# An attention and mixture kernel on one core: a new table of phase positions, and SyncE's queue for every transfer

## The chip, the core and the metric

The kernel runs on one core of one Trainium2 chip. The core has five engines with instruction streams of their own: TensorE (PE in the profile; its weight loads, PEld, overlap its products), VectorE (DVE), ScalarE (ACT), GpSimd (POOL) and SyncE (SP). Transfers are issued by an engine into a queue of its own and carried by 16 DMA engines. The metric is the device time of one execution in microseconds, as a median of several.

## The reference

A gated linear attention (4 batches, 8 heads, 768 positions, head size 48) feeds a two-matrix feed-forward with a gate:

```
scale = minimum(mag, 0.999) / (mag + 1e-6)          # mag = |a|, a = a_re + i a_im, per position and channel
for t in range(S):
    S_re, S_im = ar*S_re - ai*S_im + k[t] v[t]^T,  ar*S_im + ai*S_re
    y[t] = q[t] @ S_re
x = y, heads side by side                           # 4 x 768 x 384
xk, xr = mu * x + (1 - mu) * x_prev                 # one mu for each
v = relu(xk @ w_k)**2 @ w_v                         # 384 -> 1024 -> 384
out = sigmoid(xr @ w_r) * v                         # w_r 384 x 384
```

All is float32 at the interface; w_k, w_v and w_r arrive as eight bytes a number.

## The kernel before

The 4 x 768 positions are cut into eight units of 384, two to a batch. Each unit goes through three stages.

- `gate(u)`, on ScalarE and VectorE: it loads the unit's gates, keys and queries (g: three tiles, each of 128 channels by four rows of 384; six pieces of two rows for units 0 and 1) and its values (v, three tiles). From the gates it makes the running sum of log magnitude and of phase (`a0`, `a1`, `a2` for the magnitude: logarithms and exponentials on ScalarE, a scan, L736, on VectorE; `b0`, `b1` for the phase, with arctangent and sines). It multiplies keys and queries by both (L797). Unit 0 does that in two groups of tiles, the others in one. L719 (`a1`) is VectorE's step between two ScalarE steps on the magnitude.
- `attend(u)`, on TensorE: heads are stacked into kq by small transfers (`stack`, L834), scores (sc, L914) are masked on VectorE (pt, L923), keys transposed (tr, L865) and copied by ScalarE (kt, L871), and a state is updated (up, L885; added on VectorE, L890). The result y goes to SBUF by ScalarE (ys, L964) and by 48-row transfers to X (xt, L970, `move`).
- `mix(u)`, the feed-forward: VectorE makes the two mixtures x of neighbouring positions, TensorE the first products z (L455 for unit 0, which takes plain float32, L460 for the others, which take three products of split float32), ScalarE relu and square, its output split in hhi and hlo, and TensorE the second products o (L524, L527). The gate's z (`gate_r`) is copied by ScalarE (L478), goes through the sigmoid, is multiplied with o on VectorE (L542) and stored (L545).

The weights come in ten pieces, the first of one matrix block and the others of two (`fetch`, L380). Each is converted from its eight bytes by a step on ScalarE or VectorE (f0, L589 on ScalarE), a light pass on VectorE (L595) and a merge on VectorE (L599); `split` later divides them into the two parts that mix(1) and later units use.

The order of all this is set by a planner, class `Plan`. Each stage registers its operations with an engine, a cost in us and the buffers it uses. `due` goes over TensorE's operations sorted by a position, `at`, adds up their costs, and works back through the dependences to a due time for each operation of any engine. `run` then plays the program through: whenever an engine is free it takes, of the operations that can go, the one with the earliest due time. Instructions are emitted in that order, engine by engine, and at run time wait for one another by semaphores. When TensorE has nothing to do in the opening (from the first gate product that can't start to the first z), the planner puts fillers on it, `warm`, two matmuls each on the identity. Positions come from a table `AT` with a pair (start, end) for attend(u) and one for mix(u), in that order:

```
for u in range(NU):
    run(attend(u), *AT[2 * u])
    run(mix(u, (x0, x0_slot) if u == 0 else None), *AT[2 * u + 1])
```

so only the order of the positions over all steps matters, not their scale. Queues of transfers are engines to the planner: `SP`, SyncE's, and `GP`, GpSimd's, each with an issue cost (`QUEUE`) and, if not free at once, a time from which it is (`FREE`). `op_dma`, `op_move` and `op_dma_gp` register a transfer on SP, on whichever of both is free, or on GP.

Of the kernel before, what the change touches and what calls it, by code (L numbers as in the profile page):

```python
# [23 lines left out]
P = 128  # L24
U = 384
NC = U // P
NU = B * S // U
NT = C // P
# [13 lines left out]
CAP = 0.999  # L42


AT = ((0.42, 0.67), (2.23, 4.26), (0.93, 2.49), (2.73, 3.06), (2.24, 2.87), (3.78, 4.38), (2.83, 3.48), (4.03, 5.22),
      (3.96, 4.06), (5.16, 6.45), (5.4, 5.45), (9.16, 9.34), (6.35, 8.61), (9.06, 11.24), (9.26, 9.59), (9.6, 10.3))
PAIRS = 0, 3, 1, 2
PIECE = 2
GP = 2
# [22 lines left out]
class Plan:  # L72
# [8 lines left out]
    BEGIN = 0.8  # L81
    LATENCY = 0.16
    TABLE = 1.28
    QUEUE = dict(SP=0.63, GP=0.65)
    FREE = dict(GP=2.4, DVE=6.5)
    START, ARRIVE = 1.15, 1.3
    TURN = {("once", "half"): 0.09, ("full", "half"): 0.09,
            ("half", "once"): 0.24, ("half", "full"): 0.15}
# [189 lines left out]
def tile_kernel(ctx, tc, gat, vt, w_all, mu, slow_g, slow_v, out):  # L278
# [54 lines left out]

    def op_move(n, f, **kw):

        plan[0].op("SP", n / 220, lambda e: f(nc.sync if e == "SP" else nc.gpsimd), other={"GP": n / 220}, **kw)

    def op_dma_gp(n, f, **kw):

        plan[0].op("GP", n / 400, f, **kw)  # L340


    table(AF.Ln)
# [207 lines left out]
    with ExitStack() as fast:  # L551
# [14 lines left out]
        def fetch(i):  # L566
            s = pieces[i]
            n = s.stop - s.start

            def f():  # L570
                raws[i] = fetched(keep, s, nc.sync if i >= FETCHED else nc.gpsimd, tag=f"w{i}")[0]
            late = i >= FETCHED
            (op_dma if late else op_dma_gp)(393 * n, f, writes=[("raw", i)], reads=[("kqs", 0, ct) for ct in range(NT)] * late, bulk=late)

        def convert(i):

# [71 lines left out]
        def gate(u):  # L648
# [9 lines left out]
            def load(ct, part):  # L658
                def f():
                    if u not in G:  # L660
                        G[u] = gp.tile([P, NT, 4, U], F32, tag="g", name="g")
                    (nc.gpsimd if u == 1 else nc.sync).dma_start(out=G[u][:, ct, part], in_=gat[b, half, ct, :, part])
                key = ("in", u, ct, part.stop)
                (op_dma_gp if u == 1 else op_dma)(
                    196.6 * (part.stop - part.start), f, writes=[("g", u, ct, i) for i in range(part.start, part.stop)] + [key],
                    uses=[g_slot[u]], bulk=u >= FIRST_LOAD)

            def load_v(c):
                def f():
                    v = ap.tile([P, C + C // 2], F32, tag="v", name="v", bufs=VB)  # L670
                    (nc.sync if u else nc.gpsimd).dma_start(out=v, in_=vt[b, half, c])
                    V[u].append(v)
                (op_dma if u else op_dma_gp)(295, f, writes=[("v", u, c)], uses=[v_slot[u][c]])

            def each(c):
                return range(c.start, c.stop)
# [136 lines left out]
        def attend(u):  # L813
# [6 lines left out]
            def stack(h):  # L820
                extra = u == 0 and len(kq) - KQ
                if u == 0 and extra >= 0:

                    kq_slot[h], kq[h] = x0_slot, x0[:HR + D, NT - 2 + extra]
                else:
                    kq_slot[h] = slot("kq")
                    kq[h] = kqs[kq_slot[h][1] % KQ]
                r0, r1 = h * D, (h + 1) * D

                def move(r0, n, i):  # L830
                    def f():
                        ct, o = r0 // P, r0 - h * D
                        s = slice(r0 - ct * P, r0 - ct * P + n)
                        nc.sync.dma_start(  # L834
                            out=kq[h][i * HR + o:i * HR + o + n], in_=G[u][s, ct, 2 * i:2 * i + 2])
                    plan[0].op("SP", n * 3.07 / 220, f, reads=[("kqs" if i else "kqc", u, r0 // P)], writes=[("st", u, h, i, r0)],
                           uses=[kq_slot[h], g_slot[u]])
# [89 lines left out]
            def values(p):  # L927
# [38 lines left out]
                op_act(U + 60, out_, reads=[("y", u, p)], writes=[("ys", u, p)], uses=[sp, sy])  # L966

                def move(src, dst, i):
                    def f(queue):
                        queue.dma_start(out=X[u][dst, i, 1:U + 1], in_=t["ys", p][src])  # L970
                    k = (src.stop - src.start) * 1.54
                    (op_move if u == 0 else lambda k, f, **kw: plan[0].op("SP", k / 220, lambda: f(nc.sync), **kw))(k, f, reads=[("ys", u, p), ("X0", u)], writes=[("Xp", u, i, dst.start)],
                           uses=[sy, x_slot[u]])
# [196 lines left out]
```

## Time and profile before

| | |
|---|---|
| median of 3 runs | 432.51 us (432.43, 432.51, 433.48) |
| profiled execution, device time | 431.53 us |
| its span, first to last instruction | 429.8 us |
| mean granted TensorE clock | 0.996 |
| TensorE busy | 383.5 us (89%) |
| ScalarE, VectorE, GpSimd busy | 340.7, 332.1, 19.9 us |

The trace covers the span; the device time of the same execution is 1.7 us more. A row of time gives start, length, engine, line, operation, what is written and read, the count, and in square brackets the idle time ahead of it with what ended it. A row of a stretch gives its bounds and length, then busy time and count of PE, PEld, DVE, ACT and POOL, granted clock, the mean busy share of the DMA engines and GB/s. A row of waits gives the waiting engine, its tile and line, what it waited for, the sum in us, the count and the mean. A row of transfers has tiles, queue, count, KB each and the median us from issue to landing.

### The profile page before, as it was taken

To read this page: it belongs to the slowest core of one execution; us is meant where nothing else is said; L and a number is where in the kernel's file an instruction comes from. 1 tells how busy PE (TensorE), PEld (TensorE's weight loads), DVE (VectorE), ACT (ScalarE), POOL (GpSimd) and SP (SyncE) were. 2 spreads that over 40 slices of the span, in tenths; PEclk is the share of its full clock that TensorE was granted. 3 is DMA by queue.
4 is the path that set the end of the run, shared out by engine and by line. 5 is a ranking of instruction groups with operands and counts; after the bars stand their busy time and mean duration, and the time that the engine had idled before them with its cause. 6 is when DMAs were issued, how large, how long until landed. Compare 5 with 4: busy or idle time off the path is not lost.

```text
span 429.8 us, 9500 instructions
## 1 busy us (share of the span) xinstructions
PE 383.5 (89%) x3683; PEld 350.8 (82%) x3683; DVE 332.1 (77%) x528; ACT 340.7 (79%) x606; POOL 19.9 (5%) x59
## 2 busy tenths in 40 slices
PE   1006999999999999989999999999999999998993
PEld 1005996676679998989999999999999999998993
DVE  6699799978598989599979899696959993456322
ACT  5698769967799898899999899987998964574530
POOL 7200111000000000000000000000000200000000
PEclk9999999999999999999999999999999999999998
DMA  7946897645726737582846582388353474314001
GB/s 265 410 204 161 280 324 242 111 93 225 206 58 179 269 87 156 155 297 76 186 135 219 208 183 75 80 297 211 108 137 115 109 181 126 110 37 130 1 2 63
DMA packets 27909, 69.92 MB, mean 163 GB/s; under 512 B 5696, under 2 KB 11664, under 8 KB 27856
## 3 DMA queue, kind: packets, MB, share of 16 engines
q1 hardware_dynamic: 26320, 62.15, 49.6%
q0 software_dynamic: 1536, 7.08, 4.2%
q8 instruction: 31, 0.51, 0.5%
q14 instruction: 22, 0.18, 0.2%
HBM read 40.90 MB, written 4.72 MB: 106 GB/s over the span
## 4 chain that ended last, share of the span: by engine, by line
PE 60%; DVE 13%; issue 10%; ACT 7%; DMA 7%; POOL 2%; SPq 0%; DVEq 0%; ACTq 0%; POOLq 0%
PE z L460 23%; PE o L527 15%; PE sc L914 4%; PE y L949 4%; PE z L455 4%; PE o L524 3%; PE y L955 3%; DMA g<-in_gat 2%; PE up L885 2%; DMA kq<-g 2%; ACT sq L302 2%; DVE g L797 1%; DVE ph L764 1%; PE tr L865 1%; DMA xt<-ys 1%
## 5 line engine op out<-in xcount | busy, mean ns | idle before, releaser
L460 PE MATMUL z<-x,w 128*128 128x384 f32 x693 | 132.0, 340 | 1.2 <-ACT r L496 1.0
L460 PEld LDWEIGHTS z<-x,w 128*128 128x128 f32 x693 | 120.5, 188 | 3.3 <-issue 1.4
L527 PE MATMUL o<-hhi,w 128*128 128x384 f32 x336 | 87.5, 341 | 0.0
L527 PEld LDWEIGHTS o<-hhi,w 128*128 128x128 f32 x336 | 60.0, 188 | 1.1 <-issue 0.7
L527 PE MATMUL o<-hlo,w 128*128 128x384 f32 x168 | 56.7, 338 | 1.7 <-DVE hlo L508 1.7
L496 ACT ACTIVATE r<-z 128x384 f32<-128x384 f32 x64 | 30.8, 485 | 24.3 <-PE z L460 22.1
L865 PE MATMUL tr<-ident,g 128*128 128x128 f32 x120 | 19.2, 286 | 33.7 <-DVE g L797 33.7
L797 DVE TENSOR_TENSOR g<-g,r 128x768 f32<-128x768 f32 x48 | 43.5, 952 | 3.1 <-ACT r L302 3.0
L865 PEld LDWEIGHTS tr<-ident,g 128*128 128x128 f32 x120 | 14.2, 144 | 36.4 <-DVE g L797 34.7
L914 PEld LDWEIGHTS sc<-kq 112*64 112x64 f32 x744 | 33.5, 137 | 4.9 <-issue 2.5
L914 PE MATMUL sc<-kq 112*64 112x128 f32 (+1 forms) x744 | 36.6, 250 | 0.5 <-DMA kq<-g 0.4
L318 DVE CAST hhi<-h 128x384 fp32r<-128x384 f32 x34 | 12.2, 359 | 28.2 <-PE o L527 17.5
L500 ACT ACTIVATE h<-r 128x384 f32<-128x384 f32 x64 | 33.4, 525 | 0.7
L527 PEld LDWEIGHTS o<-hlo,w 128*128 128x128 f32 x168 | 31.5, 188 | 2.0 <-DVE hlo L508 2.0
L923 DVE TENSOR_TENSOR pt<-sc,masks 128x512 int32<-128x512 int32 x48 | 31.1, 681 | 1.6 <-PE sc L914 1.6
L302 ACT ACTIVATE sq<-m 128x1152 f32<-128x1152 f32 (+2 forms) x27 | 27.8, 1054 | 5.3 <-DVE m L745 2.8
L508 DVE TENSOR_TENSOR hlo<-h,hhi 128x384 fp32r<-128x384 f32 x56 | 30.6, 551 | 1.5 <-ACT hhi L318 0.2
L442 DVE TENSOR_TENSOR x<-xm,x 128x384 fp32r<-128x384 f32 x42 | 22.7, 552 | 10.7 <-ACT x L439 10.6
L296 ACT ACT_TABLE_LOAD x22 | 28.2, 1283 | 1.2 <-PEq L1159 0.8
L949 PE MATMUL y<-pt,v 128*48 128x128 f32 (+1 forms) x384 | 28.2, 277 | 0.2 <-DVE pt L923 0.2
L753 DVE TENSOR_TENSOR g<-g,sq 128x768 f32<-128x768 f32 x24 | 21.8, 952 | 5.4 <-ACT sq L302 5.2
L431 DVE SCALAR_TENSOR_TENSOR xm<-dx,mu_sb,xt 128x384 f32<-128x384 f32 x42 | 25.0, 614 | 0.8
(90 smaller groups left out, 657.7 us busy)
## 6 DMA issues: line engine op xcount, KB each, us to landing
g<-in_gat SPq DMA_DIRECT2D x18, 768.0 KB, 6.2
kq<-g SPq DMA_DIRECT2D x94, 144.0 KB, 3.5
again<-in_w_all SPq DMA_DIRECT2D x19, 384.0 KB, 3.3
v<-in_vt SPq DMA_DIRECT2D x21, 288.0 KB, 3.8
out_t<-zr SPq DMA_DIRECT2D x24, 192.0 KB, 2.0
raw<-in_w_all SPq DMA_DIRECT2D x5, 768.0 KB, 6.5
xt<-ys SPq DMA_DIRECT2D x45, 72.0 KB, 2.2
raw<-in_w_all POOLq DMA_DIRECT2D x4, 768.0 KB, 9.1
```

The costliest lines, as they stand in the source:

```text
L296: nc.scalar.add_instruction(mybir.InstLoadActFuncSet(name=nc.get_next_instruction_name(), act_func_set_id=loaded[0], engine=mybir.EngineTy ...
L302: nc.scalar.activation(out=out, in_=in_, func=func, **kw)
L460: nc.tensor.matmul(z, lhsT=wt[s[0]][:, part, s[1]], rhs=r[which][:, ct], start=n == 0, stop=n == 3 * NT - 1)
L496: nc.scalar.activation(out=t["r", j], in_=t["f", j], func=AF.Relu)
L500: nc.scalar.activation(out=t["h", j], in_=t["r", j], func=AF.Square)
L508: nc.vector.tensor_tensor(out=t["lo", j], in0=t["h", j], in1=t["hi", j].bitcast(F32), op=ALU.subtract)
L527: nc.tensor.matmul(tiles["o", mt], lhsT=wt[W_V + 2 * j][:, part, ts(mt, P)], rhs=r, start=j == 0 and n == 0, stop=j == NJ - 1 and n == 2)
L797: nc.vector.tensor_tensor(out=g[:, ct, 2 * i:2 * i + 2], in0=g[:, ct, 2:4], in1=t["r"][:, ct, 1 - i:2 - i].to_broadcast([P, 2, U]), op=ALU ...
L865: nc.tensor.transpose(out=t["tr", c, part][:, ct * P:(ct + 1) * P], in_=G[u][:, ct, 2 * part, c * P:(c + 1) * P], identity=ident)
L914: nc.tensor.matmul(sc[rows, i, cols], lhsT=kq[2 * p + j][:, 0, c * P + late * Q:][:, :Q], rhs=q if j else q[:, ::-1], start=True, stop=True)
L923: nc.vector.tensor_tensor(out=pts[k, c].bitcast(I32), in0=both, in1=masks.unsqueeze(1).to_broadcast([P, 2, 2, P]), op=ALU.bitwise_and)
L949: nc.tensor.matmul(t["y", p][rows, ts(c, P)], lhsT=V[u][c][:, cols], rhs=w, start=c == 0, stop=False)
```

## The change

Three things change. `AT` has other numbers, from a search over them. The queue `GP` is gone: `op_dma_gp` is removed, and its users (the g of unit 1, the v of unit 0, the first five pieces of weights) take `op_dma`, SP's. `op_move` has SP alone, so that the X transfers of unit 0, half of which GpSimd could issue, are all SyncE's. The computation is the same.

```
-AT = ((0.42, 0.67), (2.23, 4.26), (0.93, 2.49), (2.73, 3.06), (2.24, 2.87), (3.78, 4.38), ...
+AT = ((2.35, 6.85), (3.56, 5.8), (0.03, 4.77), (13.51, 15.8), (6.77, 9.94), (22.02, 23.4), ...
-    QUEUE = dict(SP=0.63, GP=0.65)
-    FREE = dict(GP=2.4, DVE=6.5)
+    QUEUE = dict(SP=0.63)
+    FREE = dict(DVE=6.5)
...
     def op_move(n, f, **kw):
-        plan[0].op("SP", n / 220, lambda e: f(nc.sync if e == "SP" else nc.gpsimd), other={"GP": n / 220}, **kw)
-
-    def op_dma_gp(n, f, **kw):
-        plan[0].op("GP", n / 400, f, **kw)
+        plan[0].op("SP", n / 220, f, **kw)
...
         def fetch(i):
...
-                raws[i] = fetched(keep, s, nc.sync if i >= FETCHED else nc.gpsimd, tag=f"w{i}")[0]
+                raws[i] = fetched(keep, s, nc.sync, tag=f"w{i}")[0]
             late = i >= FETCHED
-            (op_dma if late else op_dma_gp)(393 * n, f, writes=[("raw", i)], ...
+            op_dma(393 * n, f, writes=[("raw", i)], ...
...
             def load(ct, part):
...
-                    (nc.gpsimd if u == 1 else nc.sync).dma_start(out=G[u][:, ct, part], in_=gat[b, half, ct, :, part])
+                    nc.sync.dma_start(out=G[u][:, ct, part], in_=gat[b, half, ct, :, part])
...
             def load_v(c):
...
-                    (nc.sync if u else nc.gpsimd).dma_start(out=v, in_=vt[b, half, c])
+                    nc.sync.dma_start(out=v, in_=vt[b, half, c])
...
                 def move(src, dst, i):
-                    def f(queue):
-                        queue.dma_start(out=X[u][dst, i, 1:U + 1], in_=t["ys", p][src])
+                    def f():
+                        nc.sync.dma_start(out=X[u][dst, i, 1:U + 1], in_=t["ys", p][src])
```

After the change lines from 337 on stand four lower, those from 966 on five lower (L719 becomes L715, L1009 becomes L1004). What moves is shown at three places. In the rows, a name is the tile that is written, then `<-` and what is read.

First, the opening of the queues. Before, this is the head of SyncE's transfers (kq_97 and kq_98 are the first stacked heads):

```order
L370 DMA mu_sb<-in_mu 128x6
L662 DMA g<-in_gat 128x768 x6
L671 DMA v<-in_vt 128x576
L834 DMA kq_97<-g 48x768
L834 DMA kq_98<-g 48x768
```

and this all of GpSimd's transfers, ahead of its copies of the last position:

```order
L662 DMA g<-in_gat 128x768 x6
L671 DMA v<-in_vt 128x576 x3
L380 DMA raw<-in_w_all 128x6144 x2
L380 DMA raw<-in_w_all 128x3072
L380 DMA raw<-in_w_all 128x6144 x2
L970 DMA xt<-ys 48x384
L970 DMA xt<-ys 32x384
L970 DMA xt<-ys 16x384
L970 DMA xt<-ys 48x384 x2
L988 COPY last<-xt 128x3 x4
```

After, the head of SyncE's:

```order
L366 DMA mu_sb<-in_mu 128x6
L658 DMA g<-in_gat 128x768 x12
L376 DMA raw<-in_w_all 128x6144 x4
L376 DMA raw<-in_w_all 128x3072
L667 DMA v<-in_vt 128x576 x4
L830 DMA kq_97<-g 48x768
L830 DMA kq_98<-g 48x768
```

The twelve pieces of g stand behind each other on one queue, the five pieces of weights behind them, and the four of v, which stood ahead of the weights, behind those.

Second, ScalarE and VectorE ahead of the scans of unit 1, while TensorE works on the attention of unit 0. ScalarE before, from the first exponential of unit 1 to the step ahead of its scans:

```order
L302 ACTIVATE ph,stat<-m 128x1152
L871 COPY kt<-tr 128x8x48 x2
L715 ACTIVATE sq,stat<-ph 128x3x384
L871 COPY kt<-tr 128x8x48
L302 ACTIVATE sq<-sq 128x3x384
L871 COPY kt<-tr 128x8x48
L302 ACTIVATE sq<-m 128x3x384
L871 COPY kt<-tr 128x8x48
L302 ACTIVATE sq<-sq,consts 128x3x384
L726 ACTIVATE m<-m,consts 128x1152
```

and after:

```order
L302 ACTIVATE ph,stat<-m 128x1152
L867 COPY kt<-tr 128x8x48
L618 CAST w<-raw 128x2x384
L867 COPY kt<-tr 128x8x48
L711 ACTIVATE sq,stat<-ph 128x3x384
L302 ACTIVATE sq<-sq 128x3x384
L867 COPY kt<-tr 128x8x48 x2
L302 ACTIVATE sq<-m 128x3x384
L302 ACTIVATE sq<-sq,consts 128x3x384
L722 ACTIVATE m<-m,consts 128x1152
```

One copy of kt of five moved behind the scans' last input, none stands between the square and its logarithm any more, and a cast of a weight piece came in. VectorE before, over the same time:

```order
L703 SCALAR_TENSOR_TENSOR ph<-ph,g 128x1152
L599 SCALAR_TENSOR_TENSOR raw<-raw 128x768
L892 COPY state_95<-up 112x384
L599 SCALAR_TENSOR_TENSOR raw<-raw 128x768
L923 TENSOR_TENSOR pt<-sc,masks 128x512 x2
L719 SCALAR_TENSOR_TENSOR m<-sq,m 128x1152
L923 TENSOR_TENSOR pt<-sc,masks 128x512
L890 TENSOR_TENSOR state_96<-up,state_95 112x384
L736 SCALAR_TENSOR_TENSOR m<-m,stat,sq 128x384 x3
```

and after:

```order
L699 SCALAR_TENSOR_TENSOR ph<-ph,g 128x1152
L591 TENSOR_SCALAR raw<-raw 128x384
L621 TENSOR_TENSOR w<-raw,w 128x2x384
L595 SCALAR_TENSOR_TENSOR raw<-raw 128x384
L888 COPY state_95<-up 112x384
L715 SCALAR_TENSOR_TENSOR m<-sq,m 128x1152
L919 TENSOR_TENSOR pt<-sc,masks 128x512 x3
L886 TENSOR_TENSOR state_96<-up,state_95 112x384
L732 SCALAR_TENSOR_TENSOR m<-m,stat,sq 128x384 x3
```

Masks of scores (pt) that stood ahead of L719 stand behind it (L715 now), and two merges of weights gave way to smaller weight steps.

Third, TensorE's end, with the numbers of the tiles (o has three, one for each 128 columns; n is the one-column product of the flag that guards the slow path, and `good` comes from VectorE). Before:

```order
L527 MATMUL o_4615<-hhi_4767,w_1300 128x384 x2
L527 MATMUL o_4615<-hlo_4779,w_1300 128x384
L1041 MATMUL n_4877<-consts_82,good_4875 1x1
L527 MATMUL o_4607<-hhi_4793,w_1367 128x384 x2
L527 MATMUL o_4607<-hlo_4805,w_1367 128x384
L527 MATMUL o_4611<-hhi_4793,w_1367 128x384 x2
L527 MATMUL o_4611<-hlo_4805,w_1367 128x384
L527 MATMUL o_4615<-hhi_4793,w_1367 128x384 x2
L527 MATMUL o_4615<-hlo_4805,w_1367 128x384
```

with the last gate product z four rows ahead of the first of these. After:

```order
L523 MATMUL o_4619<-hhi_4774,w_1416 128x384 x2
L523 MATMUL o_4619<-hlo_4786,w_1416 128x384
L523 MATMUL o_4623<-hhi_4774,w_1416 128x384 x2
L523 MATMUL o_4623<-hlo_4786,w_1416 128x384
L456 MATMUL z_4822<-x_4474,w_1486 128x384 x3
L456 MATMUL z_4822<-x_4474,w_280 128x384 x6
L1036 MATMUL n_4871<-consts_82,good_4869 1x1
```

A gate product z is now the last large work of TensorE, behind the last o; the load of the flag on SyncE, `L1040 TENSOR_LOAD bad`, stands ahead of the last store, where it stood ahead of the last three.

More of the change, by code (lines that the diff above doesn't have):

```diff
@@ L42 @@
 CAP = 0.999
-AT = ((0.42, 0.67), (2.23, 4.26), (0.93, 2.49), (2.73, 3.06), (2.24, 2.87), (3.78, 4.38), (2.83, 3.48), (4.03, 5.22),
-      (3.96, 4.06), (5.16, 6.45), (5.4, 5.45), (9.16, 9.34), (6.35, 8.61), (9.06, 11.24), (9.26, 9.59), (9.6, 10.3))
+AT = ((2.35, 6.85), (3.56, 5.8), (0.03, 4.77), (13.51, 15.8), (6.77, 9.94), (22.02, 23.4), (14.62, 18.64), (22.27, 25.46),
+      (22.65, 22.92), (23.6, 25.31), (29.45, 44.63), (22.76, 34.84), (22.83, 25.16), (41.11, 56.64), (43.88, 61.13), (40.05, 48.46))
 PAIRS = 0, 3, 1, 2
@@ L570, in f @@
             def f():
-                raws[i] = fetched(keep, s, nc.sync if i >= FETCHED else nc.gpsimd, tag=f"w{i}")[0]
+                raws[i] = fetched(keep, s, nc.sync, tag=f"w{i}")[0]
             late = i >= FETCHED
-            (op_dma if late else op_dma_gp)(393 * n, f, writes=[("raw", i)], reads=[("kqs", 0, ct) for ct in range(NT)] * late, bulk=late)
+            op_dma(393 * n, f, writes=[("raw", i)], reads=[("kqs", 0, ct) for ct in range(NT)] * late, bulk=late)
         def convert(i):
@@ L661, in f @@
                         G[u] = gp.tile([P, NT, 4, U], F32, tag="g", name="g")
-                    (nc.gpsimd if u == 1 else nc.sync).dma_start(out=G[u][:, ct, part], in_=gat[b, half, ct, :, part])
+                    nc.sync.dma_start(out=G[u][:, ct, part], in_=gat[b, half, ct, :, part])
                 key = ("in", u, ct, part.stop)
-                (op_dma_gp if u == 1 else op_dma)(
+                op_dma(
                     196.6 * (part.stop - part.start), f, writes=[("g", u, ct, i) for i in range(part.start, part.stop)] + [key],
@@ L670, in f @@
                     v = ap.tile([P, C + C // 2], F32, tag="v", name="v", bufs=VB)
-                    (nc.sync if u else nc.gpsimd).dma_start(out=v, in_=vt[b, half, c])
+                    nc.sync.dma_start(out=v, in_=vt[b, half, c])
                     V[u].append(v)
-                (op_dma if u else op_dma_gp)(295, f, writes=[("v", u, c)], uses=[v_slot[u][c]])
+                op_dma(295, f, writes=[("v", u, c)], uses=[v_slot[u][c]])
             def each(c):
@@ L835, in f @@
                             out=kq[h][i * HR + o:i * HR + o + n], in_=G[u][s, ct, 2 * i:2 * i + 2])
-                    plan[0].op("SP", n * 3.07 / 220, f, reads=[("kqs" if i else "kqc", u, r0 // P)], writes=[("st", u, h, i, r0)],
+                    op_move(n * 3.07, f, reads=[("kqs" if i else "kqc", u, r0 // P)], writes=[("st", u, h, i, r0)],
                            uses=[kq_slot[h], g_slot[u]])
@@ L968, in move @@
                 def move(src, dst, i):
-                    def f(queue):
-                        queue.dma_start(out=X[u][dst, i, 1:U + 1], in_=t["ys", p][src])
-                    k = (src.stop - src.start) * 1.54
-                    (op_move if u == 0 else lambda k, f, **kw: plan[0].op("SP", k / 220, lambda: f(nc.sync), **kw))(k, f, reads=[("ys", u, p), ("X0", u)], writes=[("Xp", u, i, dst.start)],
-                           uses=[sy, x_slot[u]])
+                    def f():
+                        nc.sync.dma_start(out=X[u][dst, i, 1:U + 1], in_=t["ys", p][src])
+                    op_move((src.stop - src.start) * 1.54, f, reads=[("ys", u, p), ("X0", u)], writes=[("Xp", u, i, dst.start)],
+                            uses=[sy, x_slot[u]])
                     x_parts.setdefault(i, []).append(("Xp", u, i, dst.start))
```

## The prediction

> **What bounds the kernel now.** I read the page's busy shares first, then busy time by stretch, then what TensorE waited for once it had started, then the rows of time for the opening and the end.
>
> ```profile
> PE 383.5 (89%) x3683; PEld 350.8 (82%) x3683; DVE 332.1 (77%) x528; ACT 340.7 (79%) x606; POOL 19.9 (5%) x59
> ```
>
> ```profile
> 32.30:67.80 35.50, 31.94 (x422) 30.49 (x423) 30.69 (x42) 26.66 (x40) 4.97 (x6) 1.00 0.83 259
> ...
> 190.00:380.00 190.00, 189.62 (x1868) 181.59 (x1867) 154.38 (x257) 163.69 (x305) 3.60 (x14) 1.00 0.53 149
> 380.00:423.20 43.20, 41.55 (x237) 40.63 (x235) 19.27 (x41) 20.41 (x44) 0.00 (x0) 1.00 0.14 42
> 423.20:429.80 6.60, 0.01 (x1) 0.00 (x0) 0.67 (x2) 0.00 (x0) 0.00 (x0) 0.76 0.29 98
> ```
>
> Columns: stretch, length, busy PE, PEld, DVE, ACT, POOL, granted clock, DMA share, GB/s. TensorE has next to nothing to do before 32.3 (none of it from 4 to 20, in the stretches shown further down). From there to 67.8 it works on the attention of unit 0, and much of its busy time is fillers on the identity. After 67.8 it is dense at a granted clock of 1.00 until 423.2, and 6.6 us of end follow. Of the 355 us of the dense part only this was waiting (waits of PE from 67 us on):
>
> ```profile
> PE o L527 <- DVE hlo L508: 1.7, 1, 1.7
> PE tr L865 <- DVE g L797: 1.2, 1, 1.2
> PE z L460 <- ACT r L496: 1.0, 1, 1.0
> PE up L885 <- ACT kt L871: 0.7, 1, 0.7
> PE sc L914 <- DMA kq<-g: 0.4, 1, 0.4
> PE z L460 <- DVE pt L923: 0.3, 1, 0.3
> PE y L949 <- DVE pt L923: 0.2, 1, 0.2
> ```
>
> That is 5.5 us. So the time is: when the first product of mix(0) starts (67.89 below), plus a fixed amount of matrix work, plus those waits, plus the end. A reordering can gain on the first, the third and the fourth. The matmuls of the main path are the same in number, fillers apart.
>
> **The opening.** Rows in order of time:
>
> ```profile
> 19.58 0.55 DVE L745 TENSOR_SCALAR m<-m 128x768 f32<-128x768 f32 x1
> 21.21 0.95 ACT L589 ACTIVATE raw<-raw 128x768 int32<-128x768 uint8 x1 [2.11 <-DMA raw<-in_w_all]
> 21.21 0.56 DVE L595 TENSOR_SCALAR raw<-raw 128x768 int32<-128x768 int32 x1 [1.08 <-DMA raw<-in_w_all]
> 22.03 1.59 ACT L302 ACTIVATE sq<-m 128x768 f32<-128x768 f32 x2
> ...
> 31.29 0.96 DVE L797 TENSOR_TENSOR g<-g,r 128x768 f32<-128x768 f32 x1
> 32.27 9.39 SPq L834 DMA_DIRECT2D kq<-g  x14
> ...
> 42.43 0.48 ACT L871 COPY kt<-tr 128x384 f32<-128x384 f32 x1 [0.74 <-PE tr L865]
> 42.81 1.17 ACT L302 ACTIVATE sq<-sq 128x1152 f32<-128x1152 f32 x1
> 43.54 1.36 DVE L923 TENSOR_TENSOR pt<-sc,masks 128x512 int32<-128x512 int32 x2 [0.20 <-PE sc L914]
> 44.82 1.35 DVE L719 SCALAR_TENSOR_TENSOR m<-sq,m 128x1152 f32<-128x1152 f32 x1
> 46.20 1.17 ACT L302 ACTIVATE sq<-m 128x1152 f32<-128x1152 f32 x1 [1.86 <-DVE m L719]
> 50.07 2.84 DVE L736 TENSOR_TENSOR_SCAN m<-m,stat,sq 128x384 f32<-128x384 f32 x3 [2.83 <-ACT m L726]
> 58.63 9.42 PE L1009 MATMUL warm<-ident 128*128 128x128 f32 x82
> 66.39 2.20 DVE L421 SCALAR_TENSOR_TENSOR x<-dx,mu_sb,xt 128x384 f32<-128x384 f32 x4
> 67.89 5.97 PE L455 MATMUL z<-x,raw 128*128 128x384 f32 x18
> ```
>
> TensorE's first product of mix(0) waits for DVE (third and fourth lines from the end: half of the four x, so 67.5), and the fillers (9.42 / 82 = 0.115 us each) only fill that time. DVE and ACT in turn have two holes: 2.11 and 1.08 us for the first piece of weights at 21.21, and 2.83 us ahead of the scans at 50.07.
>
> First hole. What moved, by stretch:
>
> ```profile
> 0.00:4.00 4.00, 1.65 (x6) 1.35 (x6) 2.63 (x4) 1.28 (x1) 2.96 (x20) 1.00 0.40 94
> 4.00:8.00 4.00, 0.00 (x0) 0.00 (x0) 2.95 (x5) 2.43 (x6) 4.00 (x11) 1.00 1.01 356
> 8.00:12.00 4.00, 0.00 (x0) 0.00 (x0) 1.99 (x3) 3.39 (x9) 1.15 (x3) 1.00 1.01 393
> 12.00:16.00 4.00, 0.00 (x0) 0.00 (x0) 2.45 (x4) 3.96 (x8) 1.69 (x4) 1.00 1.03 410
> 16.00:20.00 4.00, 0.00 (x0) 0.00 (x0) 3.07 (x5) 2.00 (x5) 1.05 (x2) 1.00 1.03 401
> ```
>
> Summed, 1.8 MB by 8 us, 5.0 by 16, 6.6 by 20; the share is full from 4 us on, so only the order of the bytes can help. Before, twelve pieces of g (4.7 MB) and four of v (1.2 MB) go ahead of the first weights (0.8 MB): 6.7 MB, at 20.2 us, and the wait ends 1.0 later. Now v stands behind the weights: 5.5 MB, at 17.2 us, so the first piece is there at 18.2 and the second at 20.1. ACT then does one conversion in the hole (18.2 to 19.1) and the second, which the new order also puts ahead of the exponentials, at 20.1; these start at 21.05 instead of 22.03. Gain 1.0. DVE's weight work between its rows at 19.58 and the first g at 31.29 was, by the order, three light passes (0.56, third row), half a conversion and two merges; it is three light passes and two merges now, about 0.3 less, so I take 1.2 for everything up to the kq moves at 32.27. Bounds: 0 (the weights come no sooner) and 2.1 (the whole wait of ACT).
>
> Second hole. Two things delay ACT on its way to the scans: at 42.43 it waits 0.74 for a transpose and copies kt (0.48) ahead of the logarithm of 42.81, and at 46.20 it waits for DVE's L719, which stood behind two pt masks (43.54, 1.36 us). In the new order no kt copy stands between the square and that logarithm, which brings it about 1.1 nearer; and L719 stands ahead of all pt masks, so it starts when the logarithm ends (42.81 + 1.17 = 43.98 before) and not at 44.82: 0.8. One kt copy fewer stands between exponential and scans (0.5), and one weight CAST more (about 0.8, worked out as twice a kt copy of 384 less its fixed part) comes in ahead. Net 1.6 on top of the 1.2: scans at 47.3. From the scans to the last x that the first product needs, DVE does the same work in both orders, 17.4 us (50.07 to 67.5) without a hole. So x is ready at 64.7, and mix(0) starts at 65.0 where it started at 67.89: **gain 2.8**. TensorE's side fits: 40 fillers of two matmuls in place of 41 give 80 x 0.115 = 9.2 us from the last y of unit 0, which must end by 55.8; it ended ahead of the row at 58.63, and its masks come 2.8 sooner too. Bounds: 1.0 and 4.
>
> The X moves of unit 0, half of them by POOL, are now all by SP:
>
> ```profile
> xt<-ys SPq DMA_DIRECT2D x45, 72.0 KB, 2.2
> ...
> xt<-ys POOLq DMA_DIRECT2D x3, 72.0 KB, 3.7
> ```
>
> Six stand behind each other at 9.39 / 14 = 0.67 us of issue (a bound, those are larger), so the last is issued 2 us later than with two queues, and lands 1.5 sooner. I take 0: DVE comes to them only after masks and scans; if that cover is gone, it costs 0.5. The Trainium skill (SBUF — State Buffer, section "SBUF: two separate sides") says that a DMA of GpSimd has to wait with its descriptors while VectorE holds the port that they share, and that one of SyncE does not. By that rule the moves gain their full 1.5 and, if the path ran over them, the time would be 428; the two landing times agree with it, but not with a path there, so I give that 0.1 within my own case.
>
> **Behind the opening.** The 1.2 us of PE tr for g fall at 74, where after three z TensorE transposes the cosine and then the sine products of unit 1, six products of DVE at about 0.95. In the new order an o (2.0 us, six of 0.33 as in z's 5.97 / 18) stands between the two, and DVE mixes the products: the third cosine is its fifth. DVE ends the x at 65.0, then does a weight product (0.95), another x (2.20 / 4 = 0.55) and five products: 71.2. TensorE comes there after 5.8 us of z, at 70.8; the sines are done by 72.7, and it wants them at 73.5. About 0.3 remains: **gain 0.9**, bounds 0 and 1.2. The other 4.3 us of waits I leave as they are, since DVE reaches the products of units 3 to 7 about as much earlier as TensorE needs them; bounds 0 and 8. Changes between kinds of matmul are as many as before within a handful, at 0.1 us each: 0. Thirteen casts of hhi go from DVE to ACT; neither is the bound (154 and 164 of 190 us).
>
> **The end.**
>
> ```profile
> 418.17 0.48 ACT L478 COPY zr<-z 128x384 f32<-128x384 f32 x1 [2.10 <-PE z L460]
> 418.69 0.53 ACT L302 ACTIVATE zr<-zr 128x384 f32<-128x384 f32 x1
> ...
> 419.65 0.09 PEld L1041 LDWEIGHTS n<-consts,good 128*1 128x1 f32 x2 [0.25 <-issue]
> ...
> 422.25 1.63 DVE L542 TENSOR_TENSOR zr<-o,zr 128x384 f32<-128x384 f32 x3 [1.64 <-PE o L527]
> 422.83 1.58 SPq L545 DMA_DIRECT2D out_t<-zr  x3
> 422.87 0.34 PE L527 MATMUL o<-hlo,w 128*128 128x384 f32 x1
> ```
>
> Before, TensorE's last work is a product o, and the last multiplication ends at 423.88, 0.67 behind it. In the new order it is the last gate product z: behind it ACT copies (0.48) and takes the sigmoid (0.53), then comes the multiplication (0.55), with 0.05 between each: 1.7 behind. **Cost 1.0**, less 0.2 since the flag's small product n no longer stands ahead of the last o: 0.8. SP's load of the flag now stands ahead of the last store and waits for n; that is over within that 1.7, by bounds 0 to 0.5.
>
> **Sum**: -2.8 - 0.9 + 0.8 = -2.9 us, so 428.6 for an execution like the profiled one. The profiled execution took 431.53 (span 429.8 and 1.7 around it), 0.98 under the median of 432.51. I forecast the median: 429.6, and lower it to 429.4, since case (a) below leans that way and (b) less far the other.
>
> **Rivals.** (a) The waits of the dense part shrink as well, say the 4.3 us to under 1: about 426. For it: they are single events of 0.2 to 1.7 us in 355, each a place where one instruction stood wrongly. Against: the order is new everywhere, and can bring as many.
>
> (b) The queue brings nothing: the first weights come no sooner than 21.2, since the order gives a queue's transfers eight semaphores in turn, so that a ninth waits for the first, and sixteen at a time on two queues become eight. Then of the opening only the second hole's 1.6 remains, and the end's 0.8: 432.51 - 1.6 + 0.8 = 431.7. The Trainium skill (DMA: Bandwidth & Descriptors, section "Issuing engines are not separate DMA queues") says that all issuers share the same 16 engines, so that several save issue time only. By that rule a move to one queue is worth nothing in itself; the full shares from 4 us on agree, which is why I count the order of bytes alone.
>
> (c) Slower: DVE takes the gain back at units 4 and 5. From 190 to 380 TensorE has 0.4 us of idle and DVE is busy for 154 of 190, but in an order that waits; if the products of g for unit 4 come no earlier than before, TensorE, 3.7 us ahead, waits those 3.7 us there, and the end's 0.8 is left: 433.3. It decides from a wait of 2.9 us on, at which the opening is used up. For it speaks the cluster of small waits around unit 3 and 4, of which r and up above (1.7 together) are a part; against it, that DVE has fewer casts in its queue up to there.
>
> **Chances.** My forecast (428 to 431.1) 0.56, (a) 0.16, (b) 0.13, (c) 0.15, in which I count anything else that takes the opening's gain back. A difference under 0.3%, 1.3 us, is about what a measurement of this kernel can't tell from none: faster means under 431.2. Faster 0.72, same 0.13, slower 0.15. The range reaches from below (a) to above (b), short of (c): 425.6 to 432.5; the likeliest case alone is 428.0 to 431.1.
>
> **What would show it.** In the changed profile: the first conversion of weights at about 18 with no wait on DVE; the scans of unit 1 at about 47 to 48; the first z of mix(0) at 65, fillers ending there; under 0.5 us of PE tr waiting for g at 71; the last z 1.7 us ahead of the end of the last multiplication. It is wrong if mix(0) starts after 66.5, or if PE's waits from there on sum to more than 8 us.

## The result, and the profile after

The changed kernel takes 426.81 us in the median of six runs (425.14 to 429.77), the kernel before 432.47 (430.69 to 433.48): ratio 0.9878, 95% interval 0.9837 to 0.9919. Run again later beside other kernels it took 426.83, ratio 0.9868 (0.9839 to 0.9897). The forecast was 429.4, in a range of 425.6 to 432.5: the direction is right, and the gain of 5.7 us is nearly twice the 3.1 forecast. The time lies in the range but below the case that I held likeliest (428.0 to 431.1), 0.8 above rival (a)'s 426. One execution with ten fillers more, 459.49 us in a slower state of the chip, is left out of the medians below. The profiled execution took 426.93 with a span of 425.0, 4.8 less than the 429.8 of before.

The share of busy time hardly moved, but for GpSimd; these are the changed kernel's lines of the page, of TensorE's waits from 60 us on, and of busy time by stretch (columns as before):

```profile
PE 382.9 (90%) x3671; PEld 349.7 (82%) x3671; DVE 329.0 (77%) x515; ACT 346.0 (81%) x619; POOL 6.2 (1%) x40
```

```profile
PE o L523 <- DVE hlo L504: 1.5, 1, 1.5
PE tr L861 <- DVE g L793: 0.7, 1, 0.7
PE z L456 <- ACT kt L867: 0.3, 1, 0.3
PE sc L910 <- DMA kq<-g: 0.2, 1, 0.2
PE up L881 <- ACT kt L867: 0.2, 1, 0.2
PE o L520 <- ACT h L496: 0.2, 1, 0.2
```

```profile
4.00:8.00 4.00, 0.00 (x0) 0.00 (x0) 2.95 (x5) 2.37 (x5) 0.35 (x4) 1.00 1.03 388
8.00:12.00 4.00, 0.00 (x0) 0.00 (x0) 1.99 (x3) 3.39 (x9) 0.00 (x0) 1.00 1.03 409
...
190.00:380.00 190.00, 189.65 (x1862) 180.77 (x1862) 145.88 (x238) 163.81 (x308) 2.26 (x14) 1.00 0.52 144
...
418.20:425.00 6.80, 0.06 (x2) 0.00 (x0) 0.70 (x2) 0.97 (x2) 0.00 (x0) 0.73 0.13 42
```

TensorE's waits behind the opening are 3.1 us by these rows instead of 5.5 (3.4 with one of 0.1 at x and the digits left out): those for r and pt are gone, those for g, up and kq are smaller, the one for hlo stays, and two of 0.3 (a z behind kt) and 0.2 (h) are new. Now the opening in order of time:

```profile
17.77 0.88 ACT L585 ACTIVATE raw<-raw 128x768 int32<-128x768 uint8 x1
18.97 0.19 ACT L318 COPY stat<-m 128x2 f32<-128x2 f32 x1 [0.32 <-DVE m L732]
19.51 0.92 ACT L585 ACTIVATE raw<-raw 128x768 int32<-128x768 uint8 x1 [0.35 <-DMA raw<-in_w_all]
20.31 1.57 ACT L302 ACTIVATE sq<-m 128x768 f32<-128x768 f32 x2
...
29.05 0.95 DVE L793 TENSOR_TENSOR g<-g,r 128x768 f32<-128x768 f32 x1
30.03 2.51 SPq L830 DMA_DIRECT2D kq<-g  x4
...
46.00 2.84 DVE L732 TENSOR_TENSOR_SCAN m<-m,stat,sq 128x384 f32<-128x384 f32 x3 [1.06 <-ACT m L722]
55.09 9.20 PE L1004 MATMUL warm<-ident 128*128 128x128 f32 x80
62.16 0.56 DVE L409 TENSOR_TENSOR dx<-xt 128x384 f32<-128x384 f32 x1 [2.56 <-DMA xt<-ys]
64.12 6.35 PE L451 MATMUL z<-x,raw 128*128 128x384 f32 x18
```

The wait of 2.11 us for the first weights is gone, the exponentials start 1.7 sooner (20.31 for 22.03), the kq moves 2.2 (30.03 for 32.27), the scans 4.1 (46.00 for 50.07). Then 2.56 us go to a wait that wasn't there: VectorE stands for the X moves of unit 0. TensorE's first product of mix(0) starts at 64.12, 3.8 us sooner than the 67.89 of before. Its last product ends at about 418.2 instead of 423.2; the end behind it is as long as before, 6.8 us for 6.6.

### The profile page after: what moved, and what is told of

The parts are those of the page before. It is cut to its first block, busy times and chain, and to the rows that moved or that the text cites. A ratio compares the mean times of both kernels' runs of the same rounds, so it can differ in the third digit from the quotient of the medians.

```text
span 425.0 us, 9472 instructions
## 1 busy us (share of the span) xinstructions
PE 382.9 (90%) x3671; PEld 349.7 (82%) x3671; DVE 329.0 (77%) x515; ACT 346.0 (81%) x619; POOL 6.2 (1%) x40
## 4 chain that ended last, share of the span: by engine, by line
PE 71%; ACT 11%; DMA 7%; DVE 7%; issue 2%; SPq 1%; ACTq 0%; DVEq 0%
PE z L456 24%; PE o L523 17%; PE sc L910 6%; PE y L945 5%; PE up L881 4%; PE z L451 4%; PE y L951 4%; PE tr L861 3%; DMA g<-in_gat 3%; PE o L520 2%; DMA again<-in_w_all 1%; DMA raw<-in_w_all 1%; ACT sq L302 1%; PE warm L1004 1%; SPq L966 1%
## 5 line engine op out<-in xcount | busy, mean ns | idle before, releaser
L523 PEld LDWEIGHTS o<-hhi,w 128*128 128x128 f32 x336 | 59.7, 188 | 1.2 <-issue 0.7
L910 PE MATMUL sc<-kq 112*64 112x64 f32 (+1 forms) x744 | 36.3, 249 | 0.2 <-DMA kq<-g 0.2
L945 PE MATMUL y<-pt,v 128*64 128x128 f32 (+1 forms) x384 | 27.4, 276 | 0.0
L945 PEld LDWEIGHTS y<-pt,v 128*64 128x64 f32 (+1 forms) x384 | 21.1, 130 | 4.3 <-issue 2.5
```

The source lines that it names most:

```text
L523: nc.tensor.matmul(tiles["o", mt], lhsT=wt[W_V + 2 * j][:, part, ts(mt, P)], rhs=r, start=j == 0 and n == 0, stop=j == NJ - 1 and n == 2)
L910: nc.tensor.matmul(sc[rows, i, cols], lhsT=kq[2 * p + j][:, 0, c * P + late * Q:][:, :Q], rhs=q if j else q[:, ::-1], start=True, stop=True)
L945: nc.tensor.matmul(t["y", p][rows, ts(c, P)], lhsT=V[u][c][:, cols], rhs=w, start=c == 0, stop=False)
```

## The experiments

The edits that only move instructions were made on the finished list of the planner, just ahead of its being emitted, so that nothing else moves; `of` gives the operations that write a key, `put` moves some ahead of another. Times are medians; rows are of one execution each, which in four runs was the slowest or nearly so of its kernel (436.16 with the X moves first and fewer fillers, 432.99 with them on GpSimd, 429.00 with more fillers, 428.83 with the end and hlo).

**Queue or positions.** The first run has the changed code with the old table, the second the old code with the new one:

```
-AT = ((2.35, 6.85), (3.56, 5.8), (0.03, 4.77), ...
+AT = ((0.42, 0.67), (2.23, 4.26), (0.93, 2.49), ...
```

> The changed kernel with the old table of positions: every transfer on SyncE's queue, 41 fillers, and the old end (the last o behind the last gate product). Theory Q (the queue brings the opening: the first weights land 3.6 us sooner, since v stands behind them; the positions bring the rest): first kq move at about 30.2, first z of mix(0) at 64.5 to 66, dense part and end as before, so 429.5 to 430.5 us. Rival P (the new positions bring nearly all): first z at about 67.5 and 432 to 432.5 us. Rival W (the one queue carries more bytes in the opening but each X move then waits behind bulk pieces): weights early, but first z no sooner than 67, 431.5 to 432.5.

Measured 460.83 us, ratio 1.0658 (1.0632 to 1.0685): no theory had this. TensorE's waits from 60 us on, and three of the stretches:

```profile
PE up L881 <- ACT kt L867: 7.6, 4, 4.4
PE tr L861 <- DVE g L793: 5.1, 3, 3.9
PE o L523 <- DVE hlo L504: 3.9, 3, 2.2
PE sc L910 <- DMA kq<-g: 3.0, 5, 1.0
```

```profile
66.40:170.00 103.60, 99.92 (x866) 78.24 (x866) 87.48 (x128) 87.37 (x143) 2.11 (x1) 1.00 0.58 156
170.00:200.00 30.00, 25.57 (x312) 23.85 (x310) 26.09 (x41) 28.00 (x53) 0.00 (x0) 0.89 0.58 173
...
260.00:320.00 60.00, 51.78 (x454) 48.38 (x453) 49.47 (x74) 50.02 (x87) 0.00 (x0) 0.91 0.49 134
```

The opening gains less than theory Q had (weights at 18.1 and kq moves at 30.6 nearly as forecast, but the first z at 66.4 and not 64.5 to 66), and the waits sum to 23.8 us, single ones to 4.4. Where they are long the granted clock, as a mean over the stretch, falls to 0.89 and 0.91: 30 x 0.11 + 60 x 0.09 = 8.7 us more as an estimate. The waits of 23.8 less the 5.5 of before, and that, are 27.0 of the 29.5 by which the dense part grew (66.4 to 451.2, 384.8 for 355.3). The planner was given one queue fewer and made another order out of the same positions: of TensorE's 3545 products, fillers apart, 2424 stand at the place in its order that they had before (by the names of their tiles). Which change of the order makes the waits stays open. So the table and the queues belong together, and "the queue's gain" is no number of its own.

> The kernel before with the new table of positions, GpSimd's queue kept; the planner then puts 44 fillers ahead of mix(0). Theory Q: weights land at about 21 as before, first z at 67 to 68, TensorE's waits behind it about 3 us instead of 5.5, the end 0.2 longer: 430.5 to 432. Rival P: first z at about 65 and 427 to 428.5 us.

Measured 430.19 us, ratio 0.9941 (0.9920 to 0.9962), close to theory Q and far from P. First weights at 20.9, first z at 66.8 (1.1 sooner than before), waits 3.9 instead of 5.5, the end 7.1 us instead of 6.6. But the dense part as a whole is only 0.6 shorter (354.7 for 355.3), so the profile gives 1.1 + 0.6 - 0.5 = 1.2, by which its span of 428.6 is shorter; the other 1.1 of the 2.3 between the medians is not in this execution.

**The order of the bytes.**

```
+        order = put(of("v", 0) + of("v", 1, 0), min(of("raw"), key=order.index))
```

> The changed kernel with the four v transfers of the opening moved ahead of the five weight transfers on SyncE's queue; nothing else moves on any engine. Theory Q: four pieces of 0.75 us, so the first weights land at 20.6 instead of 17.6, the first kq move comes at 32.5 instead of 30.0, first z 2 to 2.7 us later: 428.8 to 429.5 us where the changed kernel has 426.8. Rival A (VectorE's wait of 2.56 us for the X moves ahead of mix(0) absorbs it): weights late, but first z within 0.5 us, 426.8 to 427.3.

Measured 430.01 us, ratio 0.9949 (0.9925 to 0.9973): 3.2 slower than the changed kernel. ScalarE's first conversions, and the first z:

```profile
20.83 0.88 ACT L594 ACTIVATE raw<-raw 128x768 int32<-128x768 uint8 x1 [2.79 <-DMA raw<-in_w_all]
22.73 0.95 ACT L594 ACTIVATE raw<-raw 128x768 int32<-128x768 uint8 x1 [0.94 <-DMA raw<-in_w_all]
...
66.64 5.65 PE L460 MATMUL z<-x,raw 128*128 128x384 f32 x17
```

Four transfers put ahead of five others cost 2.79 us of ScalarE at once and 2.5 at the first z. Theory Q holds, a little over its size, with an interval that just misses the changed kernel's (0.9925 against 0.9919). TensorE's and VectorE's way to the first z:

```profile
57.60 9.20 PE L1013 MATMUL warm<-ident 128*128 128x128 f32 x80
...
63.60 0.55 DVE L418 TENSOR_TENSOR dx<-xt 128x384 f32<-128x384 f32 x1
```

VectorE did absorb a part: it doesn't wait for the X moves at the second of these rows, and comes there 1.4 us later than in the changed kernel (62.16). TensorE absorbs nothing: its fillers start 2.5 later (55.09 there), and the first z stands behind them.

```
-                    nc.sync.dma_start(out=G[u][:, ct, part], ...
+                    (nc.gpsimd if u == 1 else nc.sync).dma_start(out=G[u][:, ct, part], ...
```

and in the same way for the first weights and the v behind them:

> The changed kernel with the same order of all work, but the g of unit 1, the five first weight pieces and the four v behind them issued by GpSimd, the g of unit 0 by SyncE. Theory Q (only the order of the bytes counts, as I predicted): first weights at about 18, within 0.6 of the changed kernel's 17.6, and 426.8 to 427.4 us. Rival G (GpSimd's transfers start later and are carried more slowly, 356 and 393 GB/s from 4 to 12 us against 388 and 409): first weights at 18.5 to 20, 427.7 to 429.5 us.

Measured 426.57 us, ratio 0.9863 (0.9825 to 0.9900): the changed kernel's time.

```profile
17.86 0.90 ACT L585 ACTIVATE raw<-raw 128x768 int32<-128x768 uint8 x1
19.75 0.94 ACT L585 ACTIVATE raw<-raw 128x768 int32<-128x768 uint8 x1 [0.64 <-DMA raw<-in_w_all]
```

With the bytes in the same order on two queues the first conversion starts 0.1 later, the second 0.24. Who issues is worth nothing that these runs can tell (their intervals are some 3 us wide); that v stands behind the weights is worth 3.2. With the first run of positions alone there are four times for the new table: 430.19 on two queues and 430.01 on one with v ahead, 426.57 on two and 426.81 on one with v behind. The Trainium skill (DMA: Bandwidth & Descriptors, section "Issuing engines are not separate DMA queues") has it that all issuers share the same 16 engines, and this run agrees.

**The X moves and the fillers.**

```
+        fill = [i for i in order if ops[i]["emit"] is self.fill[1]]
+        order = [i for i in order if i not in fill[-10:]]
```

> The changed kernel with ten of the forty fillers ahead of mix(0) left out (twenty matmuls on the identity, 20 x 0.115 = 2.3 us); nothing else moves. Theory X (mix(0) waits for VectorE's x, which waits 2.56 us for the X moves behind bulk pieces; the fillers only fill): TensorE's fillers end at 62.0, its first product starts then and the second waits for x at about 64.9 as now: 426.5 to 427.0 us. Rival F (the number of fillers itself holds mix(0)): first products 2 us sooner, 424.5 to 425 us.

Measured 428.51 us, ratio 0.9904 (0.9885 to 0.9924): no gain, and 1.7 behind the changed kernel's median with intervals that overlap. In its profile:

```profile
54.32 6.96 PE L1013 MATMUL warm<-ident 128*128 128x128 f32 x60
61.12 0.81 PE L460 MATMUL z<-x,raw 128*128 128x384 f32 x2
63.04 5.43 PE L460 MATMUL z<-x,raw 128*128 128x384 f32 x16 [1.11 <-DVE x L426]
```

The X moves came sooner in this execution, and the third product of mix(0), with the bulk behind it, started at 63.04, 2.0 us before the changed kernel's (65.04), as rival F had it; yet TensorE's last product ended at 418.6, 0.3 later than there. Its waits grew to 6.5 us: 1.1 for x ahead of that third product, and behind it kq (1.1 for 0.2), hhi (0.6), state (0.4) and hlo (0.4 more). An earlier start was turned into waits further on.

```
+        late = of("in", 2)[1:] + of("v", 1)[1:]
+        order = [i for i in order[:k + 1] if i not in late] + late + [i for i in order[k + 1:] if i not in late]
```

where k is the place of the last X move of unit 0:

> The changed kernel, all forty fillers kept; on SyncE's queue the second and third g of unit 2 and two v of unit 1 are moved behind the last four X moves of unit 0. Theory X with the fillers as the second bound: the X moves land at 58 to 60 instead of 61.7 to 62.5, VectorE's wait of 2.56 us goes, but the fillers still end at 64.3, so that the gain is what x waited behind them (0.1 to 0.4) and TensorE's 0.74 us for g behind it: 425.7 to 426.5. Rival B (the bulk pieces were wanted there, and their delay costs as much): 427 to 429.

Measured 431.82 us, ratio 0.9986 (0.9966 to 1.0005): 5 us slower than the changed kernel, and more than rival B had. VectorE's wait for the X moves is indeed gone, but (TensorE's waits from 66 to 100 us, and a stretch):

```profile
PE sc L926 <- issue: 1.9, 1, 1.9
PE sc L926 <- DMA kq<-g: 0.9, 3, 0.4
```

```profile
76.00:84.00 8.00, 5.17 (x65) 0.83 0.76 157
```

(The stretch is given for PE alone: busy, clock, DMA share, GB/s.) The changed kernel has 8.00 busy at a clock of 1.00 there. The row of 1.9, for which the profile names no releaser, ends at 79.21, right behind the landing of a kq move at 79.12, and the next run has 2.2 for kq at the same place. While the bulk pieces stand behind the X moves, the DMA engines run half empty, here from 56 to 60 us, the changed kernel first:

```profile
56.00:60.00 4.00, 4.00 (x39) 1.00 0.97 337
```

```profile
56.00:60.00 4.00, 4.00 (x36) 1.00 0.40 137
```

The last of the bulk pieces ahead of the kq moves of unit 1 lands at 76.1 instead of 72.1, TensorE waits 2.8 us ahead of the scores, and the clock falls to a mean of 0.83. The order that made VectorE wait 2.56 us had the cheaper of two waits.

> Both edits: ten fillers fewer and the bulk pieces behind the X moves. Theory X with both bounds: first z of mix(0) at 61.9 to 62.3 instead of 64.1, 424.0 to 425.0 us. Theory X without the fillers as a bound gives the same here but the whole gain in the run with the X moves alone; rival F gives no more than the fillers cut alone. Rival B: no gain, 426.5 or more.

Measured 433.02 us, ratio 1.0006 (0.9978 to 1.0033): rival B again. The first z came at 62.4, close to theory X, and the wait for kq took it back (2.9 us, and the clock to 0.80 in the same stretch; this is the slowest of twelve executions, 436.16).

```
+                        (nc.gpsimd if u == 0 and p in PAIRS[2:] else nc.sync).dma_start(out=X[u][dst, i, 1:U + 1], ...
```

> The changed kernel with ten fillers fewer, and the last four X moves of unit 0 issued by GpSimd instead of SyncE; the bulk pieces stay where they are, now ahead of nothing. Theory X as one of queues (a transfer waits for those ahead on its own queue): the X moves land at 59.5 to 61, first z at 62 to 63, 424.5 to 425.5 us. Rival E (it is the 16 engines that are taken, whatever the queue, as in the run with two queues in the opening): X lands no sooner than 61.5, 426.5 to 427 us.

The ten fillers are left out here too. Measured 431.49 us, ratio 0.9970 (0.9954 to 0.9987): rival E, and worse, 3.0 behind the run with fewer fillers alone.

```profile
64.87 0.56 DVE L418 TENSOR_TENSOR dx<-xt 128x384 f32<-128x384 f32 x1 [4.39 <-DMA xt<-ys]
```

On a queue of their own the X moves kept VectorE until 2.7 us later than in the changed kernel; 1.0 of that is their later issue in this execution (56.7 for 55.7). SyncE's queue no longer stops for them, so the last of the bulk pieces is issued at 57.4 instead of 62.2, and the moves share the DMA engines with all of them: they take 7.6 us to land instead of 5.5 (medians), with the engines full in both kernels. So the moves on SyncE's queue, which hold the bulk back until ys is there, seem to have worked as a brake. That GpSimd's queue is slower in itself (3.7 us for 2.2 in the kernel before) may be a part of it; no run takes the two apart.

**The changed kernel beside a later start.** The control, and ten fillers more:

> The changed kernel itself once more, so that the three edits beside it have it on the same chip: 426 to 427.5 us.

Measured 426.83 us; in its profile the first z at 64.70, and TensorE waits 2.8 us behind it, 0.4 of it for g.

> The changed kernel with ten fillers more ahead of mix(0) (twenty matmuls on the identity, 2.3 us), nothing else moved: TensorE's first z starts 2.3 us later, while VectorE and ScalarE do their work as early as before. Theory S (the time is first z plus a fixed amount, as I predicted): 2.3 us slower than the changed kernel, less at most the 1.1 us of waits at 64 to 72. Theory D (behind the opening TensorE runs into VectorE's, ScalarE's and the kq moves' pace, as the run with fewer fillers said, where 1.7 us of earlier start became waits): 0 to 1 us slower, TensorE's waits falling from 3.4 us to 1.5 or so.

Measured 427.71 us, ratio 0.9884 (0.9855 to 0.9912): 0.9 slower in the median for a first z 2.2 later (66.88). That is theory D's size, but its profile doesn't have theory D's picture: the wait for g is gone, while one of 1.2 us for a state is new, the waits sum to 3.4, and its TensorE ends 2.5 later. The control's own runs spread over 2.1 us (426.02 to 428.17), more than lies between the theories, so how much of a start is kept stays open; from the other side (ten fillers fewer) it was nothing.

**The end.**

```
+        order = put(of("z", NU - 1, NT - 1), of("o", NU - 1, NJ - 1)[0])
```

> The changed kernel with TensorE's last gate product ahead of the last o, as the kernel before had it. My prediction's term (the gate product at the end costs 0.8): 0.7 to 0.9 us faster than the changed kernel. By the two traces (the last multiplication 1.54 us behind TensorE's last product instead of 0.67, but 5.2 us from there to the end instead of 5.9, of which 0.26 are four fewer semaphores to clear and stay): 0.3 to 0.5 faster. Rival: no gain, since the flag now comes last.

Measured 427.81 us, ratio 0.9900 (0.9863 to 0.9936): no gain, the rival's case.

```profile
417.85 1.63 DVE L547 TENSOR_TENSOR zr<-o,zr 128x384 f32<-128x384 f32 x3 [5.95 <-PE o L532]
419.39 0.14 DVE L1046 TENSOR_SCALAR bad<-n 1x1 int32<-1x1 f32 x1
```

The last multiplication ends 0.67 us behind TensorE's last o, as in the kernel before, but the flag's comparison now stands behind it on VectorE, and each engine reads the flag and branches on it only then: SyncE 1.3 us behind the last multiplication, where it is 0.4 in the changed kernel. From TensorE's last main product (n left out) to the end of the span are 7.2 us, where the changed kernel has about 6.9 in both of its profiles. The last instructions of the changed kernel say why the gate product at the end was cheap (start, duration, engine, operation):

```
418.30 0.15 DVE  TENSOR_SCALAR bad<-n
418.47 0.47 SP   TENSOR_LOAD <-bad
419.24 0.56 DVE  TENSOR_TENSOR zr<-o,zr
419.87 0.07 DVE  COMPARE_BRANCH
423.39 0.02 DVE  EVENT_SEMAPHORE
419.83 0.34 SP   DMA_DIRECT2D out_t<-zr
420.23 0.05 SP   COMPARE_BRANCH
423.12 0.02 SP   EVENT_SEMAPHORE
```

Behind its branch an engine shows no instruction for 2.8 to 3.5 us. In the changed kernel the flag was computed and read while ScalarE and VectorE still worked on the last gate product.

```
+        order = put([hlo], xm)
```

(with its hhi, if that stood behind xm) beside the swap, with hlo the operation that TensorE waits for at 382 and xm the first of the two ahead of it:

> The tail swap, and VectorE's hlo of the last units for which TensorE waits 1.48 us at 382 moved ahead of the two xm in front of it (1.15 us). If TensorE is the bound there: 0.6 to 0.9 us less than the tail swap alone, the wait at 382 down to 0.6. If VectorE or ScalarE is: the wait turns up within 5 us again, as a wait for x, and the time is that of the tail swap.

Measured 425.87 us, ratio 0.9838 (0.9812 to 0.9864), 1.9 below the swap alone and 1.0 below the changed kernel run beside it. The wait at 382 fell from 1.48 to 0.42, and no wait for x follows it: TensorE was the bound there. But 1.9 is more than the 1.06 saved, and the profiled execution, the slowest of seven, doesn't show the gain: its waits elsewhere are longer (1.0 for another hlo at 281, 0.6 for kq at 78), and TensorE ends 0.6 later than with the swap alone. It is the fastest version in the median, though its interval overlaps the changed kernel's. The hlo moved beside the changed kernel's own end wasn't run.

## Why the prediction was right, and where its terms were off

- **What bounds the kernel** was right in its first part: the start of mix(0), the waits, the end. But the three aren't independent, as the sum assumed: fewer fillers made the start earlier and the waits longer. Nor do the fillers only fill time: in the kernel before, the changed kernel and the run with v ahead the first z starts as they end (by their rows at 68.05, 64.29 and 66.80; the z at 67.89, 64.12 and 66.64), and TensorE's rows show no wait for x there but for 0.11 us in the changed kernel. And the sum has no term for the clock, which by the estimate above cost 8.7 us in the run with the queue alone.
- **The first weights**: conversion at 18.2 forecast, 17.77 measured, and the run with v ahead shows the cause. The term up to the kq moves, 1.2, was 2.2: the exponentials start 0.7 sooner than forecast (20.31 for 21.05), and VectorE's way from there to the first g is 0.5 shorter (8.7 for 9.3 us), where I allowed 0.2 to 0.3.
- **The second hole**, 1.6 forecast: 4.07 less 2.24 is 1.8. Right.
- **The X moves at 0, with 0.5 if the cover is gone**: the step that failed. The cover went, and VectorE waited 2.56 us (2.0 in the second profile). I counted only the issue of six moves; what counted was the two pieces of g and one of v ahead of them. In four profiles (the changed kernel's two, v ahead, fewer fillers) the first of the four late moves lands 0.2 to 0.3 us behind that v, at 61.7, 61.6, 63.1 and 59.7. From the scans to the x I had 17.4 us without a hole; it was 18.9. The error hid itself in the sum, because the terms ahead of it were too small by 1.2 and TensorE was held by its fillers to nearly the same time: first z at 65.0 forecast, 64.1 and 64.7 measured. That part of the right time is luck.
- **TensorE's wait for g**, 0.3 forecast of 1.2: 0.7 and 0.4.
- **The other waits left as they are, 4.3 us**: 2.5 and 2.4. That is half of rival (a), which I gave 0.16, and the largest part of what the gain was more.
- **Changes between kinds of matmul at 0**: the dense part without its waits is 350.8 and 350.2 us where it was 349.8 (first z to TensorE's last product, less the waits), so 0.4 to 1.0 was lost in places that I priced at nothing; the traces don't say more.
- **The end at 0.8**: 0.2. The last multiplication is 1.66 us behind the last gate product, as forecast (1.7 for 0.67), but what follows it is 5.2 us and not 5.9: by the trace SyncE branches 0.43 behind it instead of 0.58, shows nothing for 2.8 us instead of 3.1, and has four semaphore instructions fewer behind that (16 for 20, 0.065 us each). I had taken the path to end at the multiplication. The 2.8 and 3.1 vary from profile to profile (2.8 to 3.3 in four), so a part of this may be chance.
- **Rival (b)** fell: on one queue with eight semaphores the weights came at 17.8. Who issues is worth nothing that the run with two queues could tell; the forecast counted the order of bytes, and that part paid. The rule of GpSimd's descriptors (the Trainium skill, SBUF — State Buffer, section "SBUF: two separate sides"), to which I gave 0.1, doesn't show in that run: GpSimd's weights were there within 0.24 us of SyncE's. The late landing of the X moves on GpSimd can't rule it out, since VectorE was busy until 60.5 of the 56.7 to 64.9 us that they took. **Rival (c)**: waits of its kind exist, and took all in the run with the queue alone, which was 28 us slower in place of the 3.7 of its price; but only 5.1 of its 23.8 us of waits are for the products of g, the others for kt, hlo, kq and x.

In sum, of the profile's 4.8 us: 3.8 from the start (2.8 forecast), 1.2 from the dense part (0.9), less 0.2 at the end (0.8). About 1 us of the 5.7 between the medians is not in these two executions: the one before was 0.9 under its median, the one after 0.1 above. The change as a whole is an order fitted to one queue: positions alone 2.3, v behind the weights about 3.2 on top of the new positions, and who issues 0.

## What to carry to other kernels

When queues move, look at which bytes stand ahead of which, not at who issues: here, with the new table, that was all of the queue's effect. A transfer that makes an engine wait may be the brake that lets a more urgent one through; before pulling it forward, list what then stands behind what it displaced. A table fitted to a planner holds for that planner alone: with one queue fewer the same table cost 6.6%.

## What was not expected of the hardware

- A wait of TensorE can cost more than its length, and where it falls decides. In these traces the granted clock is 1.00 or 0.50 from 60 us on and changes on a grid of 3.41 us; the 0.83, 0.89 and 0.91 above are means over both. Two steps of that grid each, at the same wait for hlo in the kernel before and in the run with the X moves on GpSimd, and at the wait for kq in the run with the X moves first:

```profile
385.70:389.11 3.41, 1.76 (x10) 1.00 0.31 71
389.11:392.52 3.41, 3.41 (x22) 1.00 0.13 49
```

```profile
385.05:388.46 3.41, 1.75 (x8) 1.00 0.00 0
388.46:391.87 3.41, 3.41 (x13) 0.50 0.08 10
```

```profile
77.87:81.28 3.41, 1.33 (x10) 1.00 0.63 129
81.28:84.69 3.41, 3.20 (x43) 0.50 0.71 184
```

From 60 us to TensorE's end, in all fourteen profiles, half clock for 3.41 or 6.83 us followed each of the eight steps at full clock in which TensorE was busy for 1.75 us or less, and none in which it was busy for 1.76 or more. As an estimate a step at half clock costs 3.41 / 2 = 1.7 us: once with the X moves first, beside 2.8 us of waiting, and five times, 8.5 us, in the run with the queue alone. No run placed a wait to test this.

- Transfers of 48 rows issued by GpSimd beside full engines took over 7 us to land (issued from 56.7, the wait for them ended at 64.9), though nothing stood ahead of them on their queue; issued by SyncE behind bulk pieces they took 5.5 in the changed kernel.
- Behind the branch on the flag VectorE and SyncE show nothing for 2.8 to 3.5 us, more than half of the 5.2 behind the last multiplication.
